# Linear attention followed by a two-layer block: query features as two 64-row products, a third feature buffer, other early loads, the last tile in two parts

## The chip, the cores and the metric

The kernel runs on one core of one Trainium2 chip. The core has TensorE (PE in the views), VectorE (DVE), ScalarE (ACT), GpSimd (POOL) and SyncE (SP), which only issues transfers here. Each engine takes its instructions in the order in which the program lists them; PE may load the weights of a later product while an earlier one runs (PEld). The metric is the device time of one execution in microseconds; the median of several runs is given.

## The reference

```python
def phi(x):
    proj = np.einsum('bhsd,df->bhsf', x, w_phi)
    proj = proj - np.max(np.abs(proj), axis=-1, keepdims=True)
    return np.concatenate([np.exp(proj), np.exp(-proj)], axis=-1)
q_p, k_p = phi(q), phi(k)
kv = np.einsum('bhsf,bhsd->bhfd', k_p, v)
z = np.sum(k_p, axis=2)
num = np.einsum('bhsf,bhfd->bhsd', q_p, kv)
den = np.einsum('bhsf,bhf->bhs', q_p, z)[..., None] + 1e-06
x = num / den            # (8, 8, 576, 64), then laid out as (8, 576, 512)
...
xn = (x - mu) / np.sqrt(var + 1e-06) * g_ln
out = x + np.maximum(xn @ w_ch1, 0.0) @ w_ch2     # 512 -> 2048 -> 512
```

There are 8 batches, 8 heads, 576 positions, head size 64, and 128 columns in w_phi. All data are float32; the kernel multiplies in bfloat16.

## The kernel before, in words

**Units and pairs.** Batches are worked in four pairs. A unit is two (batch, head) slices side by side: the first slice in partitions 0 to 63 of the transposed features, the second in 64 to 127. There are 8 units in a pair, 32 in all. In pair 0 a unit is two heads of one batch, so that batch 0 is whole after four units; in later pairs it is one head of both batches. The first 512 positions of a slice are the main part, the last 64 are the tail; tails of two slices share one tile of 128 rows, and the tails of two units are worked together (`tails`, L386).

**One unit.** Keys and queries are turned so that the head dimension lies on partitions: `qkT`, 128 rows, columns 0 to 511 queries, 512 to 1023 keys. In pair 0 PE does this (L531) and DVE or ACT copies the result; in later pairs an engine casts to `qkb` (L510) and SP issues a transposing transfer (L514). Then
- `pm` (`a_main`, L561): projections with positions on partitions, for the maxima. Each product uses 64 rows of `qkT` and 64 rows of `wbk` or `wbq`; the two slices of a unit use the upper and the lower half of the array. They are the products with `rows=True`.
- `m` (L581): DVE takes the maximum of absolute values; ACT makes `emk`, `emq` = exp of it (L597).
- `EB` (L612): ACT takes exp of plus and minus the key projections; `vv` (L626 to L635): POOL scales the values by `emk` and by its reciprocal.
- `pt` (`a_feat`, L656): query projections with features on partitions. Both products read all 128 rows of `qkT`; `wbk[:, e, :]` holds w_phi in the 64 rows of slice e and zeros in the others. ACT's exp of plus and minus gives `ea` (L662).
- `kv` (L681, L686) and `num` (L715): the two contractions; DVE forms numerator and denominator (L721 to L733), POOL divides and puts the result into `x` (L739).

**The block after it.** `x` of a pair is nine tiles of 128 rows, in three groups of three: tiles 0 to 7 are main positions, tile 8 holds both tails. DVE and ACT make mean and rstd, DVE or POOL the centred tile `xc`; it is transposed by PE in pair 0 (L923), by transfers later (L908). `hT_ps` (L973) is the first product, 16 column blocks of 4 products for each group; its relu goes to one of 32 `hT` buffers. `ch_ps` (L1005) is the second, 16 products of 512 columns for each tile; DVE scales it and adds `x` (L1012), SP stores the tile (L951; tile 8 in two transfers, L956).

**What sets the order.** `Order` is a planner that runs while the program is built. Each operation is given its engine or engines, an estimated time, what it reads and writes, and a rank. `due` walks backwards from the end and gives each operation a due time, less a lead (`early`); `run` then lets every engine take, of the operations that are ready in its own model, the one due first, and lists them in this order. PSUM's eight banks are counted as room "B". A change from full-array to 64-row products is reckoned at 0.1 us (L162). Nothing of the planner runs on the chip: it only fixes the order on each engine.

**Buffers around the change.** `ea`, `EB` and `vv` have two buffers each, `x` three (`NX`), `qkT` three, `hT` 32 (`HB`). The first loads are listed at L1081 to L1094: SP takes k of unit 0, the k tails, v of unit 0, the v tails, then k and v of unit 1; ACT takes both copies of w_phi, q of unit 0, g_ln, q of unit 1.

Of the kernel before, what the change touches and what calls it, by code (L numbers as in the profile page):

```python
# [23 lines left out]
LAG = {"PE": 0.24, "DVE": 0.20, "ACT": 0.23, "POOL": 0.22, "SP": 0.1, "DMA": 1.8, "CAST": 1.8}  # L24

# [8 lines left out]
class Order:  # L34
# [73 lines left out]
    def run(self):  # L108
        waiting, free, room, events, done = {}, {}, self.room, [], []
        rows = False  # L110
# [11 lines left out]
        while events:  # L122
# [10 lines left out]
            for engine, queue in waiting.items():  # L133
# [3 lines left out]
                while queue:  # L137
                    item = heapq.heappop(queue)
                    op = item[2]
                    if op.taken:  # L140
                        op = None
                        continue
                    if op.acquire is None or (
                        op.acquire[0] not in held and room[op.acquire[0]] >= op.acquire[1]
                    ):
                        break
                    held.add(op.acquire[0])
                    passed.append(item)
                    op = None
# [34 lines left out]
def kernel(  # L184
# [28 lines left out]
    NBUF = 3  # L213
    RN = 384
# [5 lines left out]
    NX = 3  # L220
# [21 lines left out]
    ea_bufs = [consts.tile([P, 2, MX * P], BF16, name=f"ea{i}") for i in range(2)]  # L242
# [5 lines left out]
    sched = Order({"B": 8})  # L248
# [37 lines left out]
    def dma(queue, rank, nbytes, dst, src, r=(), w=()):  # L286
# [7 lines left out]
        add(queue, {"SP": 0.55, "ACT": 0.55, "POOL": 0.84}[queue], rank, emit, r=r, w=(key, *w, *chain), lag=0.0)  # L294
        if queue == "POOL":
            add("CAST", 4.2, rank, None, r=(key,), w=w)
        else:
            add("DMA", nbytes / 340.0 / 1000.0, rank, None, r=(key,), w=w)
# [29 lines left out]
    def load_tails(t, pair, batches, queue, rank):  # L328
        key = "kqv"[0 if t is k else 1 if t is q else 2] + "x"
        for half in range(2):  # L330
            ps_ = slice(half * 64, half * 64 + 64)
            if pair == 0 and t is not q:
                (b,) = batches
                slots = range(4 * b, 4 * b + 4)
                off, step = (b * H + half) * S * D, 2 * S * D
            else:
                slots = range(H)
                off, step = (2 * pair + half) * H * S * D, S * D
            sl = slice(slots[0], slots[-1] + 1)
            if t is v:  # L340
                dst = vx_bufs[pair % 2][ps_, sl, half, 0:D]
            else:
                dst = (qx_bufs if t is q else kx_bufs)[pair % 2][ps_, sl, :]
            dma(
                queue, rank, 25000 * len(slots), dst,
                dram(t, off + 512 * D, [[D, 64], [step, len(slots)], [1, D]]),
                w=[(key, half, pair % 2, s) for s in slots],
# [156 lines left out]
    def a_trans(u, V):  # L504
        n, g = u["n"], u["g"]
        pool, tag, res = ps_B, "B", "B"
        if u["pair"]:
# [14 lines left out]
            add("SP", 1.27, V, turn, r=[("qkb", n % 2)], w=[("turn", n), *ks], lag=0.0)  # L522
            add("DMA", 1.0, V, None, r=[("turn", n), ("qkb", n % 2)], w=ks)
# [28 lines left out]
    def a_main(u, V, sides):  # L552
# [14 lines left out]
        for i in sides:  # L567
# [3 lines left out]
                + ([("EB", e, n % 2) for e in range(2)] if i else []),  # L571
# [3 lines left out]
    def a_side(u, i, V):  # L575
# [32 lines left out]
        def exps(e):  # L608
            if "EB" not in u:
                u["EB"] = att.tile([P, 2, MX, F], BF16, tag="EB", name="EB")  # L610
# [10 lines left out]
        def scale_main(t):  # L621
            if t == 1:
                u["vv"] = att.tile([P, 2, NT + 1, D1], BF16, tag="vv", name="vv")
# [17 lines left out]
        for e in range(2):  # L641
            add("ACT", 0.96, V, lambda e=e: exps(e), r=[("pm", 1, n, e), ("m", 1, n % 3, e)],
                w=[("EB", e, n % 2)], release=[("B", 1)])
        vdata = [*main_keys(u, "v"), *tail_keys(u["pair"], u["slot"], "v")]
        add("POOL", 1.5, V, lambda: scale_main(1), r=[("em", 1, n % 3), *vdata],
            w=[("vv", 1, n % 2)])
        add("POOL", 1.5, V, lambda: scale_main(0),
            r=[("en", n % 3), ("vv", 1, n % 2), *vdata], w=[("vv", 0, n % 2)])

    def a_feat(u, V):  # L650
        n = u["n"]

        def products(e):
            u["EA"] = ea_bufs[n % 2]
            u["pt", e] = ps_B.tile([P, 512], FP32, tag="B", name="pt")
            nc.tensor.matmul(  # L656
                u["pt", e], wbk[:, e, :], u["qkT"][:, 0:512], start=True, stop=True
            )
# [7 lines left out]

        for e in range(2):
            add("PE", mm(1, 512), V, lambda e=e: products(e), r=["wb", ("qkT", 0, n % NQ)],
                w=[("pt", n, e), ("EA", e, n % 2)], acquire=("B", 1))
            add("ACT", 0.96, V, lambda e=e: exps(e), r=[("pt", n, e)], w=[("EA", e, n % 2)],  # L670
                release=[("B", 1)])

    def a_kv(u, V):
# [17 lines left out]
        def copy():  # L691
# [5 lines left out]
            r=[(what, t, n % 2) for what in ("EB", "vv") for t in range(2)] + [("EBx", g % 2)],  # L697
# [84 lines left out]
    def nums(u, part, V):  # L782
        n, pair = u["n"], u["pair"]
        x = x_bufs[pair % NX]
        keys = [("EA", 0, n % 2), ("EA", 1, n % 2), ("KV", n % NKV)]
# [61 lines left out]
    def x_stats(pr, r, V):  # L847
# [38 lines left out]
        def rstd():  # L886
            sl = slice(ts[0], ts[-1] + 1)
# [7 lines left out]
    def x_trans(pr, r, slot_c, V):  # L895
# [5 lines left out]
        if pr["pair"]:  # L901
            for i in range(n):
# [10 lines left out]
                add("SP", 1.27, V, turn, r=[("xc", slot_c, i)], w=[key, *wk], lag=0.0)  # L913
                add("DMA", 0.5, V, None, r=[key, ("xc", slot_c, i)], w=wk)
# [32 lines left out]
    def store(pr, t, o):  # L947
        b0 = 2 * pr["pair"]
        if t < MX:
            b, j = b0 + t // 4, t % 4  # L950
            nc.sync.dma_start(  # L951
                out=dram(out, (b * S + j) * DM, [[4 * DM, P], [1, DM]]), in_=o
# [7 lines left out]
    HB = 2 * JC  # L960

    def moe(pr, V):
# [34 lines left out]
        def second(r, i0, n, V):  # L997
# [3 lines left out]
            def products():  # L1001
                if j0 == 0:
                    ch[t] = ps_B.tile([P, DM], FP32, tag="B", name="ch_ps")
                for jj in range(j0, j0 + n):
                    nc.tensor.matmul(  # L1005
                        ch[t], hT[r, jj][:, rt * P : (rt + 1) * P], w2_sb[:, jj, :],
# [3 lines left out]
            def result():  # L1010
                ch["o", t] = o = out_pool.tile([P, DM], FP32, tag="o", name="o")
                nc.vector.scalar_tensor_tensor(  # L1012
                    out=o, in0=ch[t], scalar=pr["rstd"][:, t : t + 1], in1=x[:, t, :],
                    op0=ALU.mult, op1=ALU.add,
# [3 lines left out]
            add("PE", mm(n, DM), V, products,  # L1018
                r=[("rstd", pair % 2, t)] + [hkey[r, jj] for jj in js]
                + [("w2", jj) for jj in (js if j0 or pair else range(JC))],  # L1020
                w=[("ch", pair, t)], acquire=("B", 1) if j0 == 0 else None)
            if j0 + n == JC:
                ok = ("o", counts["o"] % 3)
                counts["o"] += 1
                add("DVE", 0.67, V - 30.0, result,
# [216 lines left out]
```

## Time and profile before

| what | us |
|---|---|
| median of 5 runs | 383.66 |
| lowest, highest | 380.48, 385.64 |
| the profiled execution's own time | 380.71 |
| its span in the profile | 378.9 |
| PE busy | 353.1 (93%) |
| DVE busy | 277.5 (73%) |
| ACT busy | 251.2 (66%) |
| POOL busy | 205.5 (54%) |

Span is the time from the first to the last record on the core. Each row of the slices is the busy share of an engine in 40 equal parts of the span, in tenths. In a timeline a line gives start, length, engine, source line, operation, output and input, and how many instructions were merged; the length of a matmul in it includes a modelled way through the array, so neighbouring matmuls overlap, and the pace is read from the distance of starts. What stands in brackets is the engine's idle time before it and what ended it.

### The profile page before, as it was taken

To read this page: it belongs to the slowest core of one execution; us is meant where nothing else is said; L and a number is where in the kernel's file an instruction comes from. 1 tells how busy PE (TensorE), PEld (TensorE's weight loads), DVE (VectorE), ACT (ScalarE), POOL (GpSimd) and SP (SyncE) were. 2 spreads that over 40 slices of the span, in tenths; PEclk is the share of its full clock that TensorE was granted. 3 is DMA by queue.
4 is the path that set the end of the run, shared out by engine and by line. 5 is a ranking of instruction groups with operands and counts; after the bars stand their busy time and mean duration, and the time that the engine had idled before them with its cause. 6 is when DMAs were issued, how large, how long until landed. Compare 5 with 4: busy or idle time off the path is not lost.

```text
span 378.9 us, 9102 instructions
## 1 busy us (share of the span) xinstructions
PE 353.1 (93%) x3332; PEld 207.4 (55%) x3332; DVE 277.5 (73%) x722; ACT 251.2 (66%) x641; POOL 205.5 (54%) x365
## 2 busy tenths in 40 slices
PE   4667879999999999998999999999999999999994
PEld 1445656546666555654656545655565546555541
DVE  3799998999999889967689889978688785001111
ACT  3799897699879429767789548866688317433310
POOL 5689788665978548843558467844457342000000
PEclk9998899999999999999999999999999999999999
DMA  7999999968959735593737826513200136100112
GB/s 189 331 274 192 160 292 262 243 169 194 250 112 242 224 103 119 120 214 75 230 82 190 223 71 153 127 29 86 57 4 25 52 91 111 36 36 28 56 44 68
DMA packets 88605, 52.70 MB, mean 139 GB/s; under 512 B 55024, under 2 KB 83824, under 8 KB 88560
## 3 DMA queue, kind: packets, MB, share of 16 engines
q1 hardware_dynamic: 83488, 47.07, 48.1%
q0 software_dynamic: 4224, 4.19, 6.9%
q10 hardware_dynamic: 848, 0.85, 0.9%
q8 instruction: 26, 0.43, 0.5%
q14 instruction: 19, 0.16, 0.1%
HBM read 37.03 MB, written 9.44 MB: 123 GB/s over the span
## 4 chain that ended last, share of the span: by engine, by line
PE 75%; DMA 8%; ACT 8%; DVE 4%; POOL 1%; issue 1%; SPq 0%; DVEq 0%; ACTq 0%; POOLq 0%
PE ch_ps L1005 30%; PE hT_ps L973 29%; DMA qk<-in_k_dram 4%; PE pm L561 4%; PE num L715 3%; PE kv L686 3%; ACT ea L662 3%; ACT EB L612 3%; PE pt L656 2%; DVE m L581 2%; DMA qk<-in_q_dram 2%; DMA qkT<-qkb 1%; DMA kx<-in_k_dram 1%; PE kv L681 1%; PE qkT_ps L531 1%
## 5 line engine op out<-in xcount | busy, mean ns | idle before, releaser
L973 PE MATMUL hT_ps<-xT,w 128*128 128x384 bf16 x768 | 150.2, 326 | 1.4 <-ACT ea L662 0.6
L1005 PE MATMUL ch_ps<-w,hT 128*128 128x512 bf16 x576 | 148.4, 379 | 0.1
L983 ACT ACTIVATE hT<-hT_ps 128x384 bf16<-128x384 f32 x127 | 62.1, 500 | 64.3 <-PE hT_ps L973 63.8
L973 PEld LDWEIGHTS <-w 128*128 128x128 bf16 x768 | 70.9, 98 | 53.0 <-issue 2.0
L581 DVE TENSOR_REDUCE m<-pm 128x4 f32<-128x512 f32 x128 | 81.4, 679 | 6.4 <-PE pm L561 6.2
L739 POOL TENSOR_TENSOR x<-numc,rden 128x192 bf16<-128x192 f32 (+1 forms) x112 | 51.7, 472 | 58.8 <-DVE rden L733 58.4
L1005 PEld LDWEIGHTS <-hT 128*128 128x128 bf16 x576 | 52.8, 98 | 47.6 <-issue 0.3
L612 ACT ACTIVATE EB<-pm 128x512 bf16<-128x512 f32 x128 | 69.6, 626 | 8.0 <-DVE m L581 7.8
L662 ACT ACTIVATE ea<-pt 128x512 bf16<-128x512 f32 x128 | 67.2, 626 | 5.7 <-PE pt L656 5.4
L1012 DVE SCALAR_TENSOR_TENSOR o<-ch_ps,rstd,x 128x512 f32<-128x512 f32 x36 | 26.5, 743 | 52.8 <-PE ch_ps L1005 41.0
L626 POOL TENSOR_TENSOR vv<-v,emk 128x512 bf16<-128x512 f32 x32 | 34.0, 1062 | 38.5 <-ACT emk L597 26.3
L721 DVE TENSOR_TENSOR numc<-num,emq 128x195 f32<-128x195 f32 (+1 forms) x96 | 32.3, 347 | 14.0 <-PE num L715 11.5
L981 DVE TENSOR_SCALAR hT<-hT_ps 128x384 bf16<-128x384 f32 x65 | 34.6, 542 | 5.7 <-PE hT_ps L973 5.1
L715 PEld LDWEIGHTS <-ea 128*128 128x128 bf16 x512 | 28.2, 98 | 16.9 <-issue 4.8
L715 PE MATMUL num<-KV,ea 128*128 128x65 bf16 x512 | 31.3, 195 | 4.1 <-ACT KV L693 2.1
L727 DVE TENSOR_TENSOR numc<-numc,num 128x195 f32<-128x195 f32 (+1 forms) x100 | 33.3, 344 | 1.0
L626 POOL TENSOR_TENSOR vv<-v,en 128x512 bf16<-128x512 f32 x32 | 33.9, 1060 | 0.0
L561 PEld LDWEIGHTS <-qkT 64*128 64x128 bf16 x512 | 15.7, 96 | 17.9 <-issue 13.8
L858 DVE BATCH_NORM_STATS2 st<-x 128x6 f32<-128x512 bf16 x36 | 24.2, 673 | 1.2 <-POOL x L739 1.2
L686 PE MATMUL kv<-vv,EB 128*128 128x65 bf16 x512 | 24.3, 197 | 0.0
L656 PE MATMUL pt<-qkT,wbk 128*128 128x512 bf16 x64 | 23.1, 409 | 0.3 <-ACT EB L612 0.3
L686 PEld LDWEIGHTS <-EB 128*128 128x128 bf16 x512 | 22.0, 100 | 2.0 <-issue 0.2
(67 smaller groups left out, 386.0 us busy)
## 6 DMA issues: line engine op xcount, KB each, us to landing
out_dram<-o SPq DMA_DIRECT2D x32, 256.0 KB, 2.5
qk<-in_k_dram SPq DMA_DIRECT2D x28, 256.0 KB, 4.8
v<-in_v_dram SPq DMA_DIRECT2D x28, 256.0 KB, 3.6
qk<-in_q_dram SPq DMA_DIRECT2D x26, 256.0 KB, 5.2
w<-in_moe_w_ch_dram POOLq DMA_DIRECT2D x8, 512.0 KB, 8.9
qk<-in_k_dram SPq DMA_DIRECT2D x2, 512.0 KB, 6.3
qk<-in_q_dram SPq DMA_DIRECT2D x2, 512.0 KB, 7.4
v<-in_v_dram SPq DMA_DIRECT2D x2, 512.0 KB, 7.3
```

The lines of the kernel that those rows point to most:

```text
L581: nc.vector.reduce_max(out=u["m", i].rearrange("p (c e) -> p e c", e=2)[:, e], in_=u["pm", i, e], axis=AX.X, apply_absolute_value=True,)
L612: nc.scalar.activation(u["EB"][:, t, e * 4 : (e + 1) * 4].rearrange("p c f -> p (c f)"), u["pm", 1, e].rearrange("p c f -> p (c f)"), AF.E ...
L626: nc.gpsimd.tensor_tensor(out=u["vv"][:, t, 0:MX, 0:D], in0=vb[:, uu, :].rearrange("p (c d) -> p c d", d=D), in1=bcast(e[:, 0:MX], 2, D), ...
L662: nc.scalar.activation(u["EA"][:, t, e * 512 : (e + 1) * 512], u["pt", e], AF.Exp, scale=(1.0, -1.0)[t],)
L686: nc.tensor.matmul(ps[:, t, c // 4, :], EB[:, t, (c % 2) * 4 + c // 2, :], vv[:, t, c, :], start=False, stop=(t == 0 and c == MX - 1), ski ...
L715: nc.tensor.matmul(ps[:, t, i, :], lhsT, rhs, start=(j == 0), stop=(j == len(terms) - 1))
L727: nc.vector.tensor_add(out=st["numc"][:, 0:nch], in0=st["numc"][:, 0:nch], in1=st["ps"][:, 0])
L739: nc.gpsimd.tensor_tensor(out=dst, in0=st["numc"][:, i : i + cnt, 0:D], in1=bcast(st["rden"][:, i : i + cnt], 2, D), op=ALU.mult,)
L973: nc.tensor.matmul(st["ps"][:, 0:cols], w1_sb[:, kc, jj * P : (jj + 1) * P], pr["xT", r][:, kc, 0:cols], start=(kc == 0), stop=(kc == KC - 1),
L981: nc.vector.tensor_relu(h_sb[:, 0:cols], st["ps"][:, 0:cols])
L983: nc.scalar.activation(h_sb[:, 0:cols], st["ps"][:, 0:cols], AF.Relu)
L1005: nc.tensor.matmul(ch[t], hT[r, jj][:, rt * P : (rt + 1) * P], w2_sb[:, jj, :], start=(jj == 0), stop=(jj == JC - 1),)
```

## The change

1. `pt` becomes two 64-row products: product e reads only rows 64e to 64e+63 of `qkT` and of `wbk[:, e, :]`. Both are one operation for the planner, take two PSUM banks at once, and have `rows=True`.
2. The planner's PE, when its last operation was of the 64-row form, takes the next ready one of that form first if it is due less than 10 us (`STAY`) after the head of the queue.
3. `ea`, `EB` and `vv` have three buffers (`NE`), `x` two, `hT` 28.
4. Transfers of SP and ACT are counted as room "S" of eight in the planner's model.
5. The early loads are listed in another order: the second copy of w_phi on SP, k and q of unit 1 before v of unit 0 and the tails, g_ln on SP after the loads of the next two units. `load_tails` is written differently and issues the same transfers.
6. The last group of the last pair has its tiles in the order 8, 6, 7. Tile 7's second product is listed after everything else, in columns 0 to 383 and 384 to 511, each with its own PSUM bank, its own DVE operation and its own store.

```diff
+STAY = 10.0
...
-                while queue:
+                if engine == "PE" and rows:
+                    near = sorted(i for i in queue if i[2].rows and not i[2].taken)
+                    near = [i for i in near if room[i[2].acquire[0]] >= i[2].acquire[1]]
+                    if near and near[0][0] < queue[0][0] + STAY:
+                        op = near[0][2]
+                while queue and op is None:
...
+    NE = 3
...
-    NX = 3
+    NX = 2
...
-    ea_bufs = [consts.tile([P, 2, MX * P], BF16, name=f"ea{i}") for i in range(2)]
+    ea_bufs = [consts.tile([P, 2, MX * P], BF16, name=f"ea{i}") for i in range(NE)]
...
-    sched = Order({"B": 8})
+    sched = Order({"B": 8, "S": 8})
...
-        def products(e):
-            u["EA"] = ea_bufs[n % 2]
-            u["pt", e] = ps_B.tile([P, 512], FP32, tag="B", name="pt")
-            nc.tensor.matmul(
-                u["pt", e], wbk[:, e, :], u["qkT"][:, 0:512], start=True, stop=True
-            )
+        def products():
+            u["EA"] = ea_bufs[n % NE]
+            for e in range(2):
+                u["pt", e] = ps_B.tile([P, 512], FP32, tag="B", name="pt")
+            for e in range(2):
+                rows = slice(e * D, (e + 1) * D)
+                nc.tensor.matmul(
+                    u["pt", e], wbk[rows, e, :], u["qkT"][rows, 0:512], start=True, stop=True
+                )
...
+        add("PE", mm(1, 512), V, products, r=["wb", ("qkT", 0, n % NQ)],
+            w=[("pt", n, e) for e in range(2)] + [("EA", e, n % NE) for e in range(2)],
+            acquire=("B", 2), rows=True)
...
-    HB = 2 * JC
+    HB = 28
...
+        if pair == NPAIR - 1:
+            for c0, c1 in ((0, 384), (384, DM)):
+                for jj in range(0, JC, 4):
+                    second(NR - 1, LAST + jj, 4, V, c0, c1)
+                    V += 1.0
...
+    pairs[-1]["tiles"][-1] = [MX, MX - 2, MX - 1]
...
-    for half in range(2):
-        dma("ACT", 0.0, 32768, wphi_f[half * D : (half + 1) * D, :], w_phi, w=[("wphi", half)])
+    for e_, queue in enumerate(("ACT", "SP")):
+        dma(queue, 0.0, 32768, wphi_f[e_ * D : (e_ + 1) * D, :], w_phi, w=[("wphi", e_)])
     load_main(q, 0, [0], "ACT", 0.1)
-    load_tails(k, 0, [0], "SP", 0.2)
+    load_main(k, 0, [1], "SP", 0.2)
+    load_main(q, 0, [1], "ACT", 0.2)
     load_main(v, 0, [0], "SP", 0.3)
-    load_tails(v, 0, [0], "SP", 0.4)
-    dma("ACT", 0.5, 262144, gln_sb, dram(moe_g_ln, 0, [[0, P], [1, DM]]), w=["gln"])
-    load_main(k, 0, [1], "SP", 0.6)
-    load_main(q, 0, [1], "ACT", 0.6)
+    load_tails(k, 0, [0], "SP", 0.4)
+    load_tails(v, 0, [0], "SP", 0.5)
     load_main(v, 0, [1], "SP", 0.7)
...
+    dma("SP", 3.0, 262144, gln_sb, dram(moe_g_ln, 0, [[0, P], [1, DM]]), w=["gln"])
```

## The prediction

> **What bounds the kernel now.** I read the page first (shares, then the 40 slices), then busy time by stretches, then the timeline of the first 22 us, of a piece of the middle and of the end.
>
> ```profile
> PE   4667879999999999998999999999999999999994
> DVE  3799998999999889967689889978688785001111
> ACT  3799897699879429767789548866688317433310
> POOL 5689788665978548843558467844457342000000
> ```
>
> One slice is 9.5 us. TensorE (PE) is not full in the first six or seven slices and is full from there on; the other three are full in slices 2 to 7. A busy PE can still run below its rate, so I take its pace from the distances of starts.
>
> ```profile
> 30.00:40.00 10.00, 7.66 (x111) 5.75 (x106) 10.00 (x33) 9.41 (x30) 9.90 (x24) 0.84 1.10 180
> 40.00:50.00 10.00, 7.62 (x104) 5.06 (x103) 9.90 (x31) 8.30 (x23) 5.94 (x12) 0.98 0.96 172
> 280.00:300.00 20.00, 20.00 (x209) 11.67 (x208) 17.15 (x45) 13.89 (x37) 11.76 (x21) 1.00 0.08 28
> ```
>
> Columns: stretch, its length, busy PE, weight loads, DVE, ACT, POOL, granted clock, DMA share, GB/s. In pair 0's attention (to 66 us) DVE has no free time and PE a quarter of it; later PE has none, DVE some. So a PE saving counts after about 66 us, and before that only what starts DVE and ACT earlier.
>
> ```profile
> 187.08 0.59 PE L656 MATMUL pt<-qkT,wbk 128*128 128x512 bf16 x2
> 187.51 0.81 PE L1005 MATMUL ch_ps<-w,hT 128*128 128x512 bf16 x3
> 189.90 0.81 PE L973 MATMUL hT_ps<-xT,w 128*128 128x384 bf16 x4
> 190.64 0.40 PE L561 MATMUL pm<-wbk,qkT 64*128 64x128 bf16 x8
> 190.97 0.82 PE L1005 MATMUL ch_ps<-w,hT 128*128 128x512 bf16 x3
> ```
>
> First column: start. Two pt products take 187.51 - 187.08 = 0.43 us, 0.215 each. Four hT products take 0.65 where a full-array product follows (186.43 to 187.08, same timeline), but 0.74 before pm: 0.09 to enter the 64-row form. Eight pm products last 190.97 - 190.64 = 0.33; where sixteen stand together (181.82, then 182.05) eight take 0.23, so leaving costs 0.10. **One visit to the 64-row form costs 0.19 us.** Eight pm of 128 columns in 0.23 is 29 ns each, half of a full-array transpose of 128 columns (about 55): two row tiles do run side by side.
>
> ```profile
> 6.65 0.37 SPq L291 DMA_DIRECT2D qk<-in_k_dram  x1
> 11.49 1.03 PE L531 MATMUL qkT_ps<-ident,qk 128*128 128x128 bf16 x8 [1.76 <-DMA qk<-in_k_dram]
> 15.31 0.59 ACT L280 COPY qkT<-qkT_ps 128x512 bf16<-128x512 bf16 x1 [2.03 <-PE qkT_ps L531]
> 373.24 1.41 DVE L1012 SCALAR_TENSOR_TENSOR o<-ch_ps,rstd,x 128x512 f32<-128x512 f32 x2 [5.07 <-PE ch_ps L1005]
> 374.68 1.11 SPq L956 DMA_DIRECT2D out_dram<-o  x2
> ```
>
> Unit 1's keys are issued only at 6.65, behind tails and values on SP, so its transposes start at 11.49 and ACT stands 2.03 us. At the end the last ch_ps finishes at 373.85 (the run of 39 starts at 365.27 and takes 8.58); DVE, two stores and their landing fill 5.05 us to 378.9.
>
> **What the Trainium skill says.** TensorE: Matmul & The Clock Gate, Back-to-back issue gap: an isolated gap of N/2.4 + 2.5 ns, 216 for 512 columns; the trace's 215 agrees. The same page, Part 3 (Packing small matmuls), lets products on different row groups overlap with about 4 ns per added tile; pm's 29 ns agrees for 128 columns, no run here shows it for 512. TensorEngine Tiling (Array Packing), Key Properties: changing the tiling mode drains TensorE; the 0.19 us per visit is that. Perfetto Trace Analysis, Identifying the Most-Contended Engine: matmul busy share is a poor measure; hence the paces above.
>
> **The change, part by part,** against the profiled execution (span 378.9, time 380.71).
>
> 1. pt as two 64-row products (L656). Per unit two full-array products (0.43) become two side by side. Taken: 0.215 + 0.004, so 0.21 saved; the other end is nothing saved, if 512-column pairs take turns. 24 units of pairs 1 to 3 lie where PE bounds: 24 x 0.21 = **-5.0**. The 8 units of pair 0 (1.7) are covered by DVE and count nothing.
>
> 2. Visits. A pt standing alone now pays 0.19, and the stay rule pulls row work together. Counted in the order of instructions on PE, from pair 0's last pm on: before 38 visits, all pm; after 34, of which 18 hold pm with pt and 7 pt alone. 4 x 0.19 = **-0.75**.
>
> 3. Loads. On SP, the second w_phi half is new in second place, k of unit 1 third; two k-tail and two v-tail loads and v of unit 0 come after them. On ACT, q of unit 1 moves ahead, and the gln load (0.35 us of issue) leaves for SP, past all group-1 loads; its first user is the first xc, just before the xT transposes at 44.24, so tens of us cover it. Unit 1's k is issued near 1.8 instead of 6.65; at a landing of 4.8 us (page, qk loads) it is there at 6.6. ACT's 2.03 gap goes, and the first reduction starts about 0.3 earlier, since DVE no longer copies half of qkT first. Against it: the k tails land 1 to 2 us later (issued near 3, behind unit 1), so emk and POOL's first vv, at 10.34 now, come about 2.5 later; POOL then does both units without its 2.71 gap and finishes them about 1 us sooner than at 19.1. Between POOL's 1.0 and ACT's 2.3, and as DVE's own idle from 10 to 20 is 2.8, I take **-2.0**; ends +0.5 (tails decide) and -4.2 (all DVE idle from 10 to 30 goes: 2.78 + 1.42).
>
> 4. Third EA, EB and vv. They take write-after-read waits away. DVE is at 9.90 to 10.00 of 10 from 30 to 50, so they can't shorten that; 0, counted up to -1 in the end of point 3.
>
> 5. Two x buffers instead of three, 28 hT instead of 32. Pair 2 writes x where pair 0's was; in both orders of PE pair 0's last ch_ps lies near unit 17 and before pair 2's nums matter, so PE has that work to do anyway. hT of column block 12 and later needs a slot whose last reader is one step earlier. 0; each miss would cost one 0.65 hole. The DMA-slot counting adds no instruction; it only reorders SP.
>
> 6. The end. Sixteen 512-column products become 16 of 384 and 16 of 128: 16 x (0.162 + 0.055 - 0.2155) = 0.02. In the new order the last 512-column product stands 8 x 0.055 = 0.44 before the end of PE, so its DVE operation (0.67 apart in the 1.41 for two) is done 0.30 after it; the 128-column one, about 0.25 by its width, at 0.55. The store of the tile before is issued by 0.70, the last one by 1.1; the old one's second issue ended 1.94 after PE. One issue of about 0.4 replaces two of 0.55. Taken **-0.85**; ends -0.3 (small rows land slower) and -1.5.
>
> Sum: -5.0 - 0.75 - 2.0 - 0.85 = -8.6: profile 372.1. The profile lies 2.95 under the median of 383.66; with the same 8.6 the median becomes **375.1**.
>
> **Rivals.**
>
> Late transposes of unit 8 (slower). Today PE does about 10 us of work between the end of pair 0 and unit 8's pm, 20 ch_ps and 20 hT products among it; in the new order 1.7. The pm then is due near 70 - 2 = 68 (70.16 is where PE stands at that place today). Its qkT comes from a transpose issued at 64.52 that took up to 8.4 us to land: 72.9. Unmoved, PE stalls 5. For it: the q load it needs took until 60.66 in a DMA share above 1. Against: on SP the transposes now stand ahead of six group-6 loads, which held SP from 55.81 to 64.42, so they can go when the cast ends at about 61.4 and land by 66. It makes the kernel slower only if landing is 8.6 us past due, at 77 or later, with unit 9 behind it. Time then 386. Chance 0.06.
>
> No overlap for 512-column pairs: two tiles that write 512 columns each into two banks may take turns. Point 1 is then 0: 380.1. For it: no such pair is in the trace. Against: pm's 29 ns. Chance 0.09.
>
> The start gains nothing, DVE being full from 30 us and the loads of pair 1 bound by DMA up to 60.66, and new holes of 1 us appear: 375.1 + 2 + 1 = 378. Chance 0.20.
>
> More than counted: all DVE idle at the start goes (-4.2) and PE's holes after 60 (0.66, 0.55 and 1.59 in three 20 us stretches) close by half: 375.1 - 2.2 - 1.4 = 371.5. Chance 0.20.
>
> **How the numbers follow.** The forecast has 0.45, with its own range 373 to 377. A measurement here can tell about 1% (3.8 us) from no change. Faster by over 1% (below 379.8): forecast 0.45, more 0.20, no start gain 0.18, no overlap 0.02: 0.85. Within: 0.02 + 0.07 + 0.01 = 0.10. Slower: 0.05, the late transposes. The range leaves out one tenth on each side: 369.5, 2 under the best case, and 380, the no-overlap case.
>
> **What will show it.** Point 1: two pt starting together, and the next full-array product 0.22 + 0.10 = 0.32 after them, not 0.43. Point 2: 34 visits after pair 0 with "issue" gaps of weight loads. Point 3: unit 1's transposes starting near 7, no 2 us gap of ACT before 15; the first hT, 46.69 now, near 44.7. Rival one: PE idle before the first pm after pair 0, released by the transpose. Point 6: from the last product to the end about 4.2 us, not 5.05. The forecast is wrong if PE gets new holes after 66 us, most likely at unit 8 or where a turned qkT is late, as at 166 us today.

## The result, and the profile after

The changed kernel takes **380.17 us** (median of 40 runs, 378.77 to 382.08); beside it the kernel before took 383.17 (75 runs). The ratio is **0.995, 95% interval 0.9935 to 0.9965**: 1.3 to 2.5 us faster, under a third of the 8.6 forecast; 380.17 lies just outside the forecast's range (369.5 to 380). The two medians lie 3.0 apart, a little more than the ratio says. The profiled execution has a span of 378.4 us, 0.5 under that of before. A difference of two single spans is good to about 2 us only: two later kernels with the same ratio as the changed one (e3 and e11 below) had spans 1.7 and 1.5 us longer. So sizes are read from ratios, with the medians beside them where the two disagree, and causes from where a trace spends its time.

The page of the changed kernel, 40 slices of 9.5 us:

```profile
PE   2887489999999999999999999999999999999995
DVE  3879999799879768977879999976767885000102
ACT  3889589799879638876689556977779306433310
POOL 5489769889757658865456647953546432000000
```

The fifth slice of PE, a 4, and of ACT, a 5, are new: a hole near 40 us. By stretches (stretch, length, busy PE, weight loads, DVE, ACT, POOL, granted clock, DMA share, GB/s):

```profile
30.00:40.00 10.00, 7.42 (x102) 5.13 (x102) 10.00 (x35) 9.88 (x29) 9.90 (x22) 0.83 1.23 214
40.00:50.00 10.00, 5.35 (x77) 4.36 (x74) 9.54 (x23) 4.39 (x13) 5.93 (x14) 0.54 0.95 166
```

From 40 to 50 us PE is down from 7.62 to 5.35, ACT from 8.30 to 4.39, and the granted clock from 0.98 to 0.54. The middle of the timeline, at the place that the prediction showed:

```profile
187.12 0.39 PE L670 MATMUL pt<-qkT,wbk 64*128 64x512 bf16 x2
187.35 0.39 PE L572 MATMUL pm<-wbk,qkT 64*128 64x128 bf16 x8
187.57 0.39 PE L572 MATMUL pm<-wbq,qkT 64*128 64x128 bf16 x8
187.89 0.82 PE L1021 MATMUL ch_ps<-w,hT 128*128 128x512 bf16 x3
```

Two pt now take 187.35 - 187.12 = 0.23 us instead of 0.43: the pairs overlap at 512 columns too, as the prediction took it; no run before had shown it. And the end:

```profile
373.74 1.01 DVE L1029 SCALAR_TENSOR_TENSOR o<-ch_ps,rstd,x 128x512 f32<-128x512 f32 x2 [1.06 <-PE ch_ps L1021]
374.52 0.81 SPq L966 DMA_DIRECT2D out_dram<-o  x2
```

PE's last product ends at 374.15, 4.25 us before the end of the span; 4.2 was forecast, 5.05 it was.

**Work and waits.** So two predicted savings are in the trace, and the time is not. To find them I add up TensorE's work along its own order of instructions, with the paces of start to start that the prediction used (0.2155 us for 512 columns, 0.162 for 384, 0.055 for 128, 0.029 for a pm product, 0.109 for a pt in a pair, 0.031 for a num, 0.095 for each change of form). What the trace shows beyond that is called waiting here. The paces are those at the full granted clock, so time lost at a lower clock counts as waiting too; where that matters, it is said. In eleven of the traces below 41 products have no record; they are counted from the program. Up to PE's last product:

| | work | waits to 60 us | 60 to 100 | 100 to end | all waits |
|---|---|---|---|---|---|
| before | 339.7 | 29.1 | 1.9 | 3.1 | 34.1 |
| after | 332.4 | 34.0 | 2.0 | 5.7 | 41.7 |

The work fell by 7.3 us and the waits rose by 7.6; the end gave 0.8. That is the 0.5 of the spans. The gain went into two new waits: 4.9 us before 60 us, and 2.6 after 100. Of the 4.9 about 1 us at most is the clock: before 60 us it was granted at 0.50 for 6.8 us in the kernel before and for 13.7 in the changed one, over 3.4 and 4.3 us of work (an estimate from the paces above).

**The start.** Issues and first users of the early loads, from the timeline of the changed kernel:

```profile
1.87 0.58 SPq L300 DMA_DIRECT2D qk<-in_k_dram  x1
...
3.01 1.34 SPq L300 DMA_DIRECT2D kx<-in_k_dram  x2
...
8.97 0.61 PE L542 MATMUL qkT_ps<-ident,qk 128*128 128x128 bf16 x4 [1.00 <-DMA qk<-in_k_dram]
...
14.37 1.05 POOL L637 TENSOR_TENSOR vv<-v,emk 128x512 bf16<-128x512 f32 x1 [8.81 <-ACT emk L608]
```

The same POOL operation in the kernel before, and the loads of the k tails issued up to 9 us, in the kernel before and then in the changed one (KB of each, median us from issue to landing):

```profile
10.34 1.05 POOL L626 TENSOR_TENSOR vv<-v,emk 128x512 bf16<-128x512 f32 x1 [4.79 <-ACT emk L597]
...
kx<-in_k_dram SPq DMA_DIRECT2D x2, 64.0 KB, 4.6
```

```profile
kx<-in_k_dram SPq DMA_DIRECT2D x2, 64.0 KB, 6.8
```

Unit 1's k is issued at 1.87 instead of 6.65, but its transposes start only at 8.97, not near 7. Unit 0's k tails are issued behind it, at 3.01 and 3.73 instead of 1.26 and 2.06, and take longer: they land at 10.07 and 10.25 instead of 5.90 and 6.63, some 4 us later, where the prediction had 1 to 2. So they are transposed at 10.88 (6.77 before), emk of unit 0 is late, and POOL's first vv is at 14.37 instead of 10.34. The queue's own waits add one more:

```profile
SPq L300 <- DMA qk<-in_k_dram: 2.8, 1, 2.8
```

SP stood 2.8 us for that k to land before it issued the next load; from 8 to 10 us DMA moved 89 and 69 GB/s, and 154 and 282 before. The Trainium skill, DMA: Bandwidth & Descriptors, Issuing engines are not separate DMA queues, says that transfers run on the same 16 engines and interleave, whichever engine started them. That fits: for unit 1's k 7.1 us passed from issue to use, 4.84 in the kernel before.

**The hole at 40 us.** The timelines of DVE with PE, and of POOL, in the changed kernel:

```profile
40.90 2.70 DVE L881 SCALAR_TENSOR_TENSOR xc<-x,mv,gln 128x512 bf16<-128x512 bf16 x1
...
47.38 1.46 PE L938 MATMUL xT_ps<-ident,xc 128*128 128x128 bf16 x12 [4.25 <-DVE numc L742]
```

```profile
41.53 1.03 POOL L637 TENSOR_TENSOR vv<-v,en 128x512 bf16<-128x512 f32 x1
42.51 0.21 POOL L642 CAST vv<-en 128x8 bf16<-128x8 f32 x1
42.66 0.39 POOL L646 TENSOR_TENSOR vv<-vx,en 128x130 bf16<-128x130 f32 x1
```

xc takes 2.70 us; the next two of its group take 0.72 and 0.75, the longest of the others 1.57, and the first one of the kernel before took 1.06. POOL works without a pause from 39.53 to 43.0; xc ends 0.6 after it. The Trainium skill, SBUF — State Buffer, Who interferes with whom, offers the cause: a DVE instruction with two SBUF inputs contends with a POOL instruction that reads SBUF, and the ports that they share are an exclusive lock. DVE takes its work in order, so numc, which frees a PSUM bank, comes at 46.43 instead of 44.36, and PE, ACT and the first hT (50.60 instead of 46.69) wait for it.

### The profile page after: what moved, and what is told of

Its sections match the earlier page's. It is cut to its first block, busy times and chain, and to the rows that moved or that the text cites. A ratio compares the mean times of both kernels' runs of the same rounds, so it can differ in the third digit from the quotient of the medians.

```text
span 378.4 us, 9097 instructions
## 1 busy us (share of the span) xinstructions
PE 350.9 (93%) x3348; PEld 207.5 (55%) x3348; DVE 275.0 (73%) x723; ACT 251.6 (66%) x640; POOL 207.6 (55%) x368
## 4 chain that ended last, share of the span: by engine, by line
PE 65%; ACT 5%; DVE 4%; POOL 2%; issue 1%; DMA 0%; DVEq 0%; POOLq 0%
PE ch_ps L1021 27%; PE hT_ps L989 27%; PE num L730 3%; PE kv L701 3%; ACT ea L676 2%; PE pm L572 2%; ACT EB L623 2%; DVE m L592 1%; PE pt L670 1%; DVE st L873 1%; ACT hT L999 1%; PE kv L696 1%; POOL xc L891 1%; POOL xd L887 1%; DVE xc L881 1%
## 5 line engine op out<-in xcount | busy, mean ns | idle before, releaser
L1021 PE MATMUL ch_ps<-w,hT 128*128 128x512 bf16 (+2 forms) x592 | 148.6, 373 | 0.0
L999 ACT ACTIVATE hT<-hT_ps 128x384 bf16<-128x384 f32 x130 | 64.0, 502 | 63.5 <-PE hT_ps L989 63.3
L754 POOL TENSOR_TENSOR x<-numc,rden 128x192 bf16<-128x192 f32 (+1 forms) x112 | 50.5, 463 | 56.3 <-DVE rden L748 54.0
L623 ACT ACTIVATE EB<-pm 128x512 bf16<-128x512 f32 x128 | 68.5, 631 | 5.0 <-DVE m L592 4.5
L1029 DVE SCALAR_TENSOR_TENSOR o<-ch_ps,rstd,x 128x512 f32<-128x512 f32 (+2 forms) x37 | 26.7, 727 | 54.1 <-PE ch_ps L1021 42.3
L637 POOL TENSOR_TENSOR vv<-v,emk 128x512 bf16<-128x512 f32 x32 | 33.5, 1047 | 37.6 <-ACT emk L608 24.4
L997 DVE TENSOR_SCALAR hT<-hT_ps 128x384 bf16<-128x384 f32 x62 | 32.9, 542 | 2.8 <-PE hT_ps L989 2.5
L742 DVE TENSOR_TENSOR numc<-numc,num 128x195 f32<-128x195 f32 (+1 forms) x100 | 33.5, 343 | 0.7
L730 PE MATMUL num<-KV,ea 128*128 128x65 bf16 x512 | 32.2, 198 | 1.9 <-ACT EB L623 1.0
L572 PEld LDWEIGHTS <-qkT 64*128 64x128 bf16 x512 | 17.2, 99 | 13.4 <-issue 7.3
L887 POOL TENSOR_TENSOR xd<-x,mv 128x512 f32<-128x512 bf16 x17 | 18.8, 1105 | 9.9 <-DVE mv L874 8.2
```

Source lines behind the costliest of these rows:

```text
L623: nc.scalar.activation(u["EB"][:, t, e * 4 : (e + 1) * 4].rearrange("p c f -> p (c f)"), u["pm", 1, e].rearrange("p c f -> p (c f)"), AF.E ...
L637: nc.gpsimd.tensor_tensor(out=u["vv"][:, t, 0:MX, 0:D], in0=vb[:, uu, :].rearrange("p (c d) -> p c d", d=D), in1=bcast(e[:, 0:MX], 2, D), ...
L730: nc.tensor.matmul(ps[:, t, i, :], lhsT, rhs, start=(j == 0), stop=(j == len(terms) - 1))
L742: nc.vector.tensor_add(out=st["numc"][:, 0:nch], in0=st["numc"][:, 0:nch], in1=st["ps"][:, 0])
L754: nc.gpsimd.tensor_tensor(out=dst, in0=st["numc"][:, i : i + cnt, 0:D], in1=bcast(st["rden"][:, i : i + cnt], 2, D), op=ALU.mult,)
L997: nc.vector.tensor_relu(h_sb[:, 0:cols], st["ps"][:, 0:cols])
```

## The experiments

**Theory 1**: what the pairs save is real, but the new loads hold up the start, and the rest is lost in waits that ACT, DVE and POOL end. **Rivals**: the pairs save nothing; one part alone (the stay rule, the third buffers, an unlucky order) is to blame. "Same order" below means that the order of instructions on every engine is that of the kernel named; otherwise the planner made a new one. Waits are in the table's columns; all comparisons are with the kernel before, which the changed kernel leads by 0.995.

| run | ratio to before (95%) | work | to 60 | 60-100 | 100-end |
|---|---|---|---|---|---|
| e1_full_pt | 0.9967 (0.9947-0.9988) | 337.5 | 34.0 | 1.9 | 3.0 |
| e2_pool_after_xc | 0.9917 (0.9894-0.9939) | 332.4 | 33.5 | 2.1 | 5.6 |
| e3_query_first | 0.9953 (0.9932-0.9974) | 332.2 | 35.8 | 2.1 | 5.7 |
| e4_only_pt_pairs | 1.0061 (1.0036-1.0086) | 337.1 | 29.0 | 6.8 | 3.6 |
| e5_old_loads | 0.9868 (0.9825-0.9910) | 332.5 | 28.8 | 5.1 | 5.6 |
| e6_new_loads_alone | 1.0228 (1.0182-1.0274) | 339.0 | 33.8 | 7.1 | 3.7 |
| e7_no_stay | 1.0020 (0.9998-1.0042) | 337.7 | 34.1 | 2.1 | 4.1 |
| e8_two_buffers | 1.0184 (1.0142-1.0227) | 332.7 | 33.5 | 5.7 | 10.2 |
| e9_k_tails_first | 0.9865 (0.9819-0.9911) | 332.0 | 28.6 | 5.4 | 5.5 |
| e10_wphi_split | 0.9896 (0.9852-0.9940) | 332.4 | 29.1 | 7.3 | 5.8 |
| e11_jitter | 0.9953 (0.9932-0.9974) | 332.4 | 35.4 | 2.1 | 5.7 |
| e12_old_loads_full_pt | 0.9869 (0.9829-0.9908) | 337.8 | 28.0 | 3.7 | 3.0 |
| e13_act_light | 0.9887 (0.9855-0.9920) | 332.4 | 32.5 | 2.1 | 3.9 |
| e14_dve_light | 0.9855 (0.9818-0.9891) | 332.4 | 31.9 | 2.2 | 2.8 |
| e15_both_light | 0.9798 (0.9763-0.9833) | 332.4 | 32.8 | 2.1 | 1.8 |

In four of these executions the granted clock stood at 0.50 for 3.4 us between 60 and 100 us: e4, e5, e6 and e10. Over 1.4 to 1.8 us of work that is about as much in their column 60-100 that is no wait for another engine. In the kernel before, the changed kernel and e1 the clock is full from 60 us on.

**e1: the pairs taken back, in the same order.**

```
-                    u["pt", e], wbk[rows, e, :], u["qkT"][rows, 0:512], start=True, stop=True
+                    u["pt", e], wbk[:, e, :], u["qkT"][:, 0:512], start=True, stop=True
```

> The changed kernel in exactly its own order of instructions, but with pt as two full-array products (128 rows of wbk and qkT, as in the kernel before). Theory 1 (the pairs overlap, and what they save is real where TensorE is the bound): the 24 units of pairs 1 to 3 cost 0.21 us more each, less what the 2.9 us of new PSUM waits after unit 8 absorb: +3 to +5 us over the changed kernel, ratio to the kernel before 1.003 to 1.008. Rival (the pairs save nothing, or their saving turns wholly into waiting): no change from the changed kernel, 0.993 to 0.997.

Measured 0.9967: 0.7 us slower by the ratio (1.5 by the medians), and not 3 to 5. From unit 8's first pm to PE's end the work is 4.16 us more (24 x 0.213, less five visits to the 64-row form that fall away), the waits are 4.2 instead of 7.0, the elapsed time 1.3 more. No order has changed and both traces have the full clock there, so it is shown: two thirds of what the pairs save comes back as waiting. Each theory held half: the saving is real, the time isn't.

**e2: xc kept clear of POOL, in the same order.**

```
+            if u["n"] == 5 and t == 0:
+                nc.gpsimd.tensor_copy(out=hold_sb, in_=pairs[0]["xc", 0][:, 0, 0:1])
             nc.gpsimd.tensor_tensor(
```

> The changed kernel in its own order, with one POOL copy of a 128 x 1 piece of pair 0's first xc tile put ahead of unit 5's first vv, so that POOL waits for that xc. Theory 1 (DVE's xc took 2.70 us because POOL's vv operations held it up): xc takes under 1.5 us, the first hT product comes about 1.2 us earlier than 50.60, and the time falls by 0.8 to 1.5 us (ratio to before 0.988 to 0.991). Rival (xc is slow for another reason, or the stage is bound by DVE's sum of work, so a delay there moves nothing): the time within 0.3 us of the changed kernel, 0.994 to 0.996.

Timeline of this run, POOL and DVE:

```profile
42.24 0.74 DVE L884 SCALAR_TENSOR_TENSOR xc<-x,mv,gln 128x512 bf16<-128x512 bf16 x1
43.05 0.19 POOL L639 COPY hold<-xc 128x1 bf16<-128x1 bf16 x1 [0.75 <-DVE xc L884]
43.19 1.04 POOL L640 TENSOR_TENSOR vv<-v,en 128x512 bf16<-128x512 f32 x1
```

xc takes 0.74 us, the first hT comes at 49.94, the ratio is 0.9917: 1.3 us faster by the ratio, within the 0.8 to 1.5 expected, but 0.4 by the medians, and the two intervals touch; the first hT gained 0.7 and not 1.2. That POOL's operations stretch xc is shown. What it costs is 0.4 to 1.3 us of the start's 4.9.

**e3: unit 0's query products ahead of unit 1's keys, all else in the same order** (one entry of TensorE's list moved behind the two that follow it).

> The changed kernel with one step of TensorE's order moved: unit 0's query products (pm) and pt come before unit 1's k transposes, which wait for the late k load until 8.97. Theory 1 (the early loads gain nothing since k of unit 1 lands late, and TensorE stands for it in order): DVE's gap of 0.85 at 10 us and ACT's of 1.41 at 11 us shrink by 1 us together, the first hT moves by 0 to 0.7 us, and so does the time: 0.993 to 0.995. Rival (the whole loss at the start is this one wait): first hT about 2 us earlier, time -2 us, 0.990 or less.

0.9953, no change: PE's standing for unit 1's k is not what the start costs. The rival falls. Of theory 1 the time came true, the first hT did not: it came at 51.80, 1.2 us later. In this execution unit 0's q landed late, too (PE turned it at 7.48, 6.08 in the changed kernel), so its start tells little.

**e4: the kernel before with pairs alone.** Its two pt entries become one:

```
+        add("PE", mm(1, 512), V, products, r=["wb", ("qkT", 0, n % NQ)],
+            w=[("pt", n, e) for e in range(2)] + [("EA", e, n % 2) for e in range(2)],
+            acquire=("B", 2), rows=True)
```

> The kernel before with one part of the change alone: pt as two 64-row products recorded as row-tiled work that takes two PSUM banks at once; loads, buffers and the end as before, the order planned anew. Theory 1 (pairs save 0.21 us each in 24 units, but banks taken in twos bring waits of 2 to 3 us): faster by 2 to 5 us, 0.987 to 0.995, with PE's holes after unit 8 at 5 us or more (4.1 in the kernel before). Rival (the early loads and the extra buffers cause the new waits, not the pairs): faster by the whole 5 to 6 us, 0.985 to 0.987, with holes as in the kernel before.

Slower, 1.0061: both expectations missed. The pairs save 6.8 us in 32 units, but without the stay rule TensorE visits the 64-row form 75 times instead of 53 (after unit 8 alone 22 of its visits are for a lone pt), 22 x 0.19 = 4.2 us back; the work falls by 2.6, the waits rise by 5.3, of which about 1.4 is the clock.

**e5: the changed kernel with the old early loads.**

```
-    load_main(k, 0, [1], "SP", 0.2)
-    load_main(q, 0, [1], "ACT", 0.2)
+    load_tails(k, 0, [0], "SP", 0.2)
...
+    load_main(k, 0, [1], "SP", 0.6)
+    load_main(q, 0, [1], "ACT", 0.6)
```

> The changed kernel with the early loads of the kernel before (unit 1's k and q behind the k and v tails, gln on ACT), the order planned anew. Measured so far: what TensorE waits up to unit 8's first pm is 30.0 and 30.3 us in the two kernels with the old loads, 34.2 to 36.6 in four with the new. Theory 1 (the new loads cost the start some 4 us): 30 to 31 us of waits up to unit 8, time 3 to 4 us under the changed kernel, 0.984 to 0.988 of before. Rival (the stay rule and the pairs make the start slow, whatever the loads): waits of 34 us or more, time as the changed kernel, 0.993 to 0.998.

0.9868, 3.1 us faster than the changed kernel (medians: 2.0), and waits to 60 us of 28.8: theory 1. From 60 to 100 us 3.1 of the 5.2 us that the start gains is given back, about 1.5 of it to the clock, which stood at 0.50 from 76.7 to 80.1 us. This run, and below it e12, which had the full clock there (the number after POOL's count):

```profile
76.60:80.20 3.60, 3.60 (x13) 1.33 (x12) 3.23 (x7) 3.53 (x10) 3.52 (x6) 0.53 1.31 242
```

```profile
76.60:80.20 3.60, 3.17 (x17) 1.64 (x17) 3.60 (x9) 3.60 (x11) 3.52 (x6) 1.00 0.87 174
```

**e6: the new early loads alone, in the kernel before** (the reverse edit, with gln moved as in the change).

> The kernel before with the new order of the early loads alone, planned anew. Theory 1: waits of TensorE up to unit 8 rise from 30.0 to 33 or more and the time by 3 to 4 us, ratio 1.007 to 1.012. The prediction's own step, that these loads save 2 us: 0.994. Rival (they are neutral, the start being bound by DVE): 0.998 to 1.002.

1.0228, 8.7 us slower: theory 1's sign, at twice its size. The prediction's step, -2.0, is refuted in this kernel, in a new order.

**e7: without the stay rule.**

```
-STAY = 10.0
+STAY = -1e9
```

> The changed kernel without the rule by which TensorE stays in row work (STAY so low that it never applies), planned anew. Theory 1 (pairs pay only with the rule, as visits of pt alone cost 0.19 us each: the kernel before with pairs alone had 57 visits after unit 8 and not 33): 50 to 60 visits, 4 us more work, time 3 to 6 us over the changed kernel, 1.003 to 1.011. Rival (the rule itself makes the PSUM waits, by heaping pm and pt): more visits, but waits after unit 8 fall from 7.0 to 4 us, time within 1 us of the changed kernel.

78 visits instead of 50, 5.3 us more work, waits after unit 8 down from 7.0 to 5.4: 1.002, 2.7 us slower than the changed kernel, a little less than expected. The rule is what makes the pairs bearable.

**e8: two EA, EB and vv buffers.**

```
-    NE = 3
+    NE = 2
```

> The changed kernel with two EA, EB and vv buffers instead of three, planned anew. The prediction priced the third buffers at nothing: waits after unit 8 within 1 us of 7.0, time within 1.5 us of the changed kernel, 0.991 to 0.999. Rival (three buffers are what lets ACT and TensorE run ahead): slower by 3 us or more, 1.003 and up.

1.0184: the prediction's price of nothing is wrong by some 9 us in this kernel. POOL shows one place of it; this run first, then the changed kernel:

```profile
25.36 0.51 POOL L754 TENSOR_TENSOR x<-numc,rden 128x192 bf16<-128x192 f32 x1 [5.50 <-DVE rden L748]
```

```profile
24.78 0.51 POOL L754 TENSOR_TENSOR x<-numc,rden 128x192 bf16<-128x192 f32 x1 [1.41 <-DVE rden L748]
```

With two buffers POOL makes four vv halves, stands 5.5 us, and takes up x; with three it makes a third unit's vv in that time. e6, which has two buffers as well, stands 5.4 us at the same place. So the late start seems to cost some 9 us with two buffers (e6) and 3 with three (e9 below); each of these kernels has an order of its own.

**e9: k tails ahead of unit 1's k, all else as changed.**

```
+    load_tails(k, 0, [0], "SP", 0.2)
-    load_main(k, 0, [1], "SP", 0.2)
+    load_main(k, 0, [1], "SP", 0.25)
...
-    load_tails(k, 0, [0], "SP", 0.4)
```

> The changed kernel with one pair of loads moved: the k tails of unit 0 are issued ahead of unit 1's k instead of behind it and v; all else as in the changed kernel, planned anew. Theory 1a (the new loads hurt since the tails come late, and POOL's first vv with them): POOL's first vv near 10 to 11 us and not 14.4, waits of TensorE up to unit 8 of 30 to 31.5, time 3 to 4 us under the changed kernel, 0.984 to 0.988. Theory 1b (they hurt since unit 1's main loads take DMA time from unit 0's v and the tails together): waits of 33 or more, time within 1.5 us of the changed kernel.

Timeline of this run:

```profile
1.88 1.32 SPq L300 DMA_DIRECT2D kx<-in_k_dram  x2
3.24 0.61 SPq L300 DMA_DIRECT2D qk<-in_k_dram  x1
...
10.84 1.05 POOL L637 TENSOR_TENSOR vv<-v,emk 128x512 bf16<-128x512 f32 x1 [5.29 <-ACT emk L608]
```

POOL starts at 10.84, waits to 60 us are 28.6, the ratio is 0.9865, 3.3 us (medians: 2.4) faster than the changed kernel. Unit 1's transposes start at 9.21, issued 1.4 us later and used 0.24 later. So it is theory 1a: with the k tails in front, the rest of the new loads, gln late on SP among it, costs nothing that these runs show. This is, with e5 and e12, the fastest full kernel here.

**e10: old loads, but w_phi on two queues** (the e5 kernel with that one line of the change).

> The changed kernel with the old order of the k, q and v loads, but with the two halves of w_phi on two queues and gln late on SP, as the change has them. DVE waited 1.3 us for w_phi with both halves on ACT, and 0.3 with them split. Theory 1 (w_phi and gln are the harmless part of the new loads): 0 to 1 us under the run with all old loads, 0.984 to 0.987, waits up to unit 8 of 28 to 30. Rival (gln behind the group-1 loads delays the first xc, or w_phi's half on SP delays the k tails enough to count): 0.990 or more.

The kernel that ran is not quite the one described: gln is on ACT, as in the kernel before, and issued at 3.63 us. So this run tries w_phi alone; gln late stands in e9. 0.9896 lies between the two expectations; against e5 the intervals overlap, so whether w_phi's second queue costs anything stays open.

**e11: a control of the planner.**

```
-    E_ATT, E_X, E_MOE, E_W, E_X0, E_M0, E_S0 = 8.0, 4.0, 0.0, 25.0, 25.0, 10.0, 0.0
+    E_ATT, E_X, E_MOE, E_W, E_X0, E_M0, E_S0 = 8.0, 4.2, 0.0, 25.0, 25.0, 10.0, 0.0
```

> A control: the changed kernel with one constant of the planner altered by little (how early the work of the tails is due, 4.2 for 4.0), which exchanges places in 118 of the 618 DVE rows and adds, drops or moves no load and no kind of work. It shows what a new order alone is worth. Theory 1 holds if it stays within 1.5 us of the changed kernel (0.991 to 0.999), so that 3 us and more in the other replanned runs is their edit and not luck. Rival (orders differ by several us by luck): 2 us or more to either side.

0.9953, no change. TensorE's order changed in 42 of 3348 places, all in its first fifth, so this control is weak: it says that small exchanges cost nothing, not what a wholly new order would do.

**e12: e5's kernel in its own order, pt as full-array products** (the edit of e1).

> The run with the old loads in exactly its own order, with pt as full-array products: the test of the pairs again, in a kernel whose start is not held up. In the changed kernel this cost 4.2 us of work after unit 8, of which 2.8 disappeared in waits. If waits that ACT and DVE end absorb it (theory 1): 0.5 to 2 us over the run with the old loads, 0.988 to 0.992, with waits after unit 8 down from 10.5 to 7.5 or so. Rival (the absorption was peculiar to that order): the whole 4 to 5 us, 0.997 to 1.000, with waits still 10.

0.9869 against 0.9868: no difference, with six runs each and intervals of 1.5 us to either side. After unit 8 the work is 4.16 us more and the waits are 6.45 instead of 10.5. So 4.0 of 4.16 is gone; but about 1.5 of e5's 10.5 is the clock, which leaves some 2.5 for absorption, near the 2.8 of e1. Not peculiar to one order, then.

**e13, e14, e15: who ends these waits?** In the same order, less to do for ACT, for DVE, for both (half of the exponentials of pt and half of the maxima are left out; e13 and e15 have six more POOL operations at the very start, which set the columns of EA that ACT leaves):

```
-                    u["EA"][:, t, e * 512 : (e + 1) * 512], u["pt", e], AF.Exp,
+                    u["EA"][:, t, e * 512 : e * 512 + 256], u["pt", e][:, 0:256], AF.Exp,
...
-                in_=u["pm", i, e], axis=AX.X, apply_absolute_value=True,
+                in_=u["pm", i, e][:, :, 0 : F // 2], axis=AX.X, apply_absolute_value=True,
```

> The changed kernel in exactly its own order, with ACT's exponentials of pt made on 256 of 512 columns (the other columns of EA are set once at the start): half of what ACT does for EA is left out, some 30 us of 252, and each PSUM bank of pt comes free about 0.5 us sooner. Not a unit of TensorE's or DVE's work changes. Theory 1 (what the pairs save is lost as TensorE runs into PSUM banks that ACT has still to read): waits of TensorE after unit 8 fall from 7.0 to 5 us or less, time 1.5 to 3 us under the changed kernel, 0.986 to 0.991. Rival (DVE's reads of num and pm, or the order of the instructions, end the waits): waits 6 us or more, time within 1 us, 0.992 to 0.996.

> The changed kernel in exactly its own order, with DVE's maxima of pm taken over 64 of each 128 columns: half of these columns are left out, 0.3 of 0.68 us in 128 operations, some 35 us of DVE's 275; TensorE and ACT do all they did. Theory 1 (the waits after unit 8 are ended mostly by ACT): waits after unit 8 fall by no more than 1.5 us; at the start, where DVE is busy at over 9 of 10 from 30 to 50 us, the first hT comes 2 us or more sooner, time 2 to 4 us under the changed kernel. Rival (DVE ends them): waits after unit 8 down to 4.5 or less.

> Both of these: ACT's exponentials of pt on half of the columns, and DVE's maxima over half of them, in the changed kernel's own order. Theory 1 (TensorE waits for the readers of its PSUM banks, whoever they are): the two gains about add up, waits after unit 8 of 4 us or less, as with the full-array pt. Rival (the remaining waits are of the order itself, or of TensorE's own pace): no better than the better one of the two.

ACT's 128 operations went from 628 to 404 ns, DVE's from 679 to 412. Waits after unit 8: 7.0, then 4.7 with ACT light, 4.0 with DVE light, 2.3 with both. e13 came as theory 1 had it. e14 went to the rival: DVE ends as many of these waits as ACT; its start gained 1.65 us at the first hT, not 2. e15 shows that they add up (2.3 + 3.0 forecast 5.3, measured 4.7). TensorE's waits by what ended them, from 73 us on, in the changed kernel and then in e15:

```profile
PE pm L572 <- DVE numc L742: 0.7, 1, 0.7
PE hT_ps L989 <- ACT EB L623: 0.7, 2, 0.4
PE kv L696 <- DVE m L592: 0.6, 1, 0.6
PE xT_ps L410 <- ACT ea L676: 0.5, 1, 0.5
PE pm L572 <- ACT ea L676: 0.3, 1, 0.3
...
```

```profile
PE ch_ps L1021 <- issue: 0.5, 3, 0.2
PE hT_ps L989 <- DVE m L592: 0.4, 1, 0.4
PE hT_ps L989 <- ACT hT L999: 0.3, 1, 0.3
```

The list of the changed kernel comes to 3.2 of the 7.0 us; what makes the rest it does not show. pm reads nothing that numc makes, hT nothing of EB, kv nothing of m. All of these products take a bank of the one pool of eight, and numc, EB, m and ea are the readers that give one back. The Trainium skill, Perfetto Trace Analysis, Matmuls, asks for rotating banks so that ACT and DVE empty one while the next is filled; this kernel does, and the trace shows the limit: TensorE comes round before its readers are done. With both lighter, the waits on numc, EB and ea are gone. That readers end these waits is shown; that it is for a bank is read from the program, as no run has another number of banks.

## Why the prediction was wrong

- **Point 1, pt pairs (-5.0): mechanism and pace right, the step after it wrong.** 0.23 us for two, 4.16 us less work after unit 8 net of visits. The step that failed is in the first part: "later PE has none, DVE some. So a PE saving counts after about 66 us". A PE that is busy throughout is not one that waits for nobody: in e1 and e12 2.8 and about 2.5 of these 4.16 us come back, at waits whose ends ACT and DVE set. Worth in time: 0 to 1.5 us. The prediction priced a faster TensorE against what DVE and ACT had free on average, and never asked when the banks come back.
- **Point 2, visits (-0.75): right as work**, 38 visits after unit 8 became 33, 0.95 us. As a part of the change it is worth more: without the rule the pairs bring 60 visits (e7).
- **Point 3, early loads (-2.0): the step that failed worst.** "at a landing of 4.8 us ... it is there at 6.6" was a landing of 7.1 us, at 8.9; and the late k tails, seen ("POOL's first vv ... come about 2.5 later", measured 4.0), were put below ACT's gap. It lies outside its own ends of +0.5 and -4.2: waits to 60 us rose by 4.9, and e9, e5 give 3.1 to 3.3 us of time back (medians: 2.0 to 2.4) with the k tails in front. A load moved ahead was priced; the loads it moved past, on a shared set of DMA engines and on a queue that then stood 2.8 us, were not.
- **Point 4, third buffers (0): the term put at nothing that was worth most, some 9 us in the changed kernel** (e8, in an order of its own). "DVE is at 9.90 to 10.00 of 10 from 30 to 50, so they can't shorten that" looked only at DVE; POOL's 5.5 us before 25 us and the waits after 100 us (10.2 against 5.7) are elsewhere. e12 says the same from another side: with full-array pt and the old loads it is 5.0 us faster than the kernel before. The end gives 0.8 of that; the other 4 belong to the buffers, the fewer visits (43 for 53 in all) and the new order, and of these the prediction had priced only the visits, at 0.75.
- **Point 5, x and hT buffers and the room "S" (0)** were not tried alone; what they cost or gave stays open.
- **Point 6, the end (-0.85): right**, -0.8.

Of the rivals, "the start gains nothing ... and new holes of 1 us" came nearest, with its signs right and both sizes too small. No overlap is refuted by the trace, late transposes of unit 8 too: its pm, due near 68 by the prediction, ran at 73.53, earlier than before (76.18), with no wait of PE on a transpose just ahead of it.

What stays open: why 60 to 100 us takes more waits once the start is mended: 3.4 us in e9 at the full clock, and in e5 and e10 1.6 and 3.8 besides what the clock makes. From 70 to 80 us of e9 DVE is busy 9.97 and ACT 9.62 of 10, and PE's waits there end with both; it was not tested. And how much of e4, e6 and e8 belongs to their edit and how much to a new order, since the control hardly moved TensorE's order.

## What to carry to other kernels

Before a saving on the busiest engine is counted, list its in-order waits and who ends them: with PSUM banks shared by all stages, a TensorE at 98% can hand a 4 us saving straight to the readers of its banks, and here lighter readers took most of those waits away (7.0 to 2.3 us). An early load is a reordering of all loads behind it: follow the one that starts the slowest chain (here the 64 KB k tails, not the 256 KB keys). And keep an instruction order fixed while one operand form changes: that run separates work from waits when two whole kernels can't. Compare the granted clock of the same stretch as well: 3.4 us at 0.50 made 1.5 us look like waiting.

## What the hardware showed that was not expected

One DVE operation, xc, of 0.74 us when POOL waited (e2), took 2.70 under six POOL operations in a row (2.69 in e1, at the same place). In e4 it took 2.00, and there a POOL cast that began within it took 0.72 us instead of 0.21: each side was held up.

The granted clock stood at 0.50 from 40.8 to 51.0 us of the changed kernel. It fell some 2 us ahead of PE's wait of 4.25 us, so that wait did not bring it down. What runs in such a stretch is slower: eight kv products took 0.46 us from start to start (49.18 to 49.64), and 0.26 in the kernel before at the full clock (42.90 to 43.16).
